# Block-diagonal v for the strided heads of an attention and expert kernel

## Chip, cores and metric

The kernel runs on one core of a Trainium2 chip. The time is device microseconds of one execution, and the median of several runs counts. Engines are called as in the profile: PE is TensorE (PEld its weight loads), DVE VectorE, ACT ScalarE, POOL GpSimd, SP SyncE, which here issues most DMAs.

## What is computed

Attention over 4 sequences of 576 positions with 8 heads of 64 (4 heads with a local mask of 32 positions, 4 with a strided mask), then a layer that sends each of the 2304 tokens to one of 8 experts, then a dense feed-forward layer:

```python
mask_local = (rel >= 0) & (rel < stride)
mask_strided = (rel >= 0) & (pos[None, :] % stride == pos[:, None] % stride)
masks = np.stack([mask_local if h < H // 2 else mask_strided for h in range(H)], axis=0)
scores = np.where(masks[None, :, :, :], scores, -1000000000.0)
...
x = np.ascontiguousarray(attn_out.transpose(0, 2, 1, 3)).reshape(B * S, H * D)
x = _moe_ref(x=x, **moe_kwargs)
return _moe2_ref(x=x, **moe2_kwargs)
```

All matmuls of the attention are in f32.

## The kernel before

The attention stage is one loop over 40 units, `for k in range(NU)` in `attention_and_routing`: 22 units of the strided heads, then 18 of the local ones. A pass k of the loop works on several units at once, as in a pipeline. It makes the scores of unit k (`stage_s`: mask matmuls, line 194, and score matmuls, line 207), the transposes of the probabilities of unit k-2 (`stage_t`, 236), the matmuls with v of unit k-3 (`stage_v`, 253 strided, 264 local), on DVE the division by the sums of unit k-4 (`v_norm1` to `v_norm3`) and the transposes of the result of unit k-5 (`stage_x`, 317). From pass 29 on the gate products of two tiles of tokens are added (`products`, 358). PE takes these in the order of the code.

A strided unit has 2 groups of 54 positions (`SR`; 3 columns of 18 positions that see each other) and 4 heads, which stand as two pairs `pr` with two heads `par` each. The transposed probabilities `pt` hold the keys of pair 0 in rows 0 to 63 and those of pair 1 in rows 64 to 127. `stage_v` runs one matmul for every `par`, `pr` and group: 54 rows, 64 columns of PE, 65 columns of v (64 and a column of ones that gives the sum).

Ahead of the scores of a unit stand matmuls on a tile `warm` whose result nobody reads (line 192): `KEEP0` gives their number for passes 0 to 10, `KEEP` that for later ones, 1 for a strided unit and 0 for a local one.

q with k, and v, come in by DMAs that SP issues in the order of the code, one of each for a group of one or two units (`load_qk`, `load_v`, called by `loads_to`, at every pass for `NLD - 1` groups ahead). A DMA waits until its buffer is free, and those behind it on SP wait too. POOL clears `x2t`, loads the constants of the routing (`load_consts`, called in pass 3) and then stores the strided results to DRAM (`store`, 310); the local results are stored by SP (302) once all loads are issued. Behind the loop come the routing, the experts and the feed-forward layer, which the change leaves alone.

Of the kernel before, what the change touches and what calls it, by code (L numbers as in the profile page):

```python
# [8 lines left out]
F32 = mybir.dt.float32  # L9
# [10 lines left out]
NE, FF, F2 = 8, 1024, 2048  # L20
# [20 lines left out]
NCV = 4  # L41
XR = 4
KEEP_R = (7, 9, 9)
NXN = 15
ST0 = 12
KEEP_D = 2
KEEP_X = 5
EARLY0 = (0, 0)
NOH = (3, 7)
QB = 32  # L50
QL = 2 * 256 + 2 * (256 + QB)
KEEP = {"s": 1, "l": 0}
KEEP0 = {0: 0, 1: 4, 2: 4, 3: 4, 4: 4, 5: 4, 6: 3, 7: 3, 8: 3, 9: 2, 10: 2}
NWM = 4
NLD = 9
NWS = 3
N_LOC = 8

# [27 lines left out]
def attention_and_routing(es, tc, a, x1, res):  # L86
    nc = tc.nc
    sy, ac, ve, gp, pe = nc.sync, nc.scalar, nc.vector, nc.gpsimd, nc.tensor
# [3 lines left out]
    cst = es.enter_context(tc.tile_pool(name="a_cst", bufs=1))  # L92
    ld = es.enter_context(tc.tile_pool(name="a_ld", bufs=NLD))
    wk = es.enter_context(tc.tile_pool(name="a_wk", bufs=3))
# [20 lines left out]
    mloc = cst.tile([128, 3, 64], BF16, name="mloc")  # L115
    mstr = cst.tile([128, 64], BF16, name="mstr")
    wg = cst.tile([128, 4, 32], F32, name="wg")
    fold = cst.tile([128, NE], F32, name="fold")
# [9 lines left out]
    groups, gof = [], {}  # L128
    for kind, sizes in (("s", (1, 1, 1, 1) + (2,) * 9), ("l", (2,) * 9)):
        t0 = 0  # L130
# [4 lines left out]
    for gi, (kind, t0, n) in enumerate(groups):  # L135
        for t in range(t0, t0 + n):
            gof[kind, t] = (gi, t - t0)
    qk_t, v_t = {}, {}

    def load_qk(gi):  # L140
        kind, t0, n = groups[gi]
        t = ld.tile([128, QL], F32, tag="qk", name="qk")
        if kind == "s":
            sy.dma_start(out=t[:, 0:n * 4 * SU], in_=a["qks"][:, t0:t0 + n, :].rearrange("p t c -> p (t c)"))
        else:
            sy.dma_start(out=t, in_=a["qkl"][:, t0 // 2, :])
        qk_t[gi] = t

    def load_v(gi):
        kind, t0, n = groups[gi]  # L150
        v = ld.tile([128, 4, 4, 66], F32, tag="v", name="v")
        vf = v.rearrange("p i h d -> p (i h d)")
        if kind == "s":
            sy.dma_start(out=vf[:, 0:264 * n], in_=a["vs"][:, t0:t0 + n, :].rearrange("p t c -> p (t c)"))
        else:
            sy.dma_start(out=vf[:, 0:528 * n], in_=a["vl"][:, 4 * t0:4 * t0 + 4 * n, :].rearrange("p i c -> p (i c)"))
        v_t[gi] = v

# [2 lines left out]
    def loads_to(k):  # L161
        while ngl[0] <= min(k, len(groups)):
            gi = ngl[0]
            if gi < len(groups):
                load_qk(gi)
            if gi > 0:
                load_v(gi - 1)
            ngl[0] += 1

    def geom(k):  # L170
        kind, t = units[k]
        gi, o = gof[kind, t]
        if kind == "s":
            return kind, t, 128 if t < NST - 1 else 64, 64, gi, o
        return kind, t, 128, 64, gi, o

    st = {}

    def sgroups(t):
        return [(g, min(SR, NT - t * SU - g * SR)) for g in range(2) if t * SU + g * SR < NT]  # L180

    def stage_s(k):
# [7 lines left out]
        mk = mk.unsqueeze(1).to_broadcast([128, 2, w])  # L190
        for i in range(KEEP0.get(k, KEEP[kind])):
            pe.matmul(sp[:, i % 2, 256:512], lhsT=warm[:, 0:128], rhs=warm[:, 0:256], start=True, stop=True)
# [23 lines left out]
    def v_max(k):  # L216
        kind, t, n, w, gi, o = geom(k)
        mx = wk.tile([128, 2, 2], F32, tag="mx", name="mx")
        ve.tensor_reduce(out=mx[0:n], in_=st[k, "s"], axis=AX.X, op=ALU.max)
        st[k, "m"] = mx  # L220
# [20 lines left out]
    def stage_v(k, xp=None):  # L241
        kind, t, n, w, gi, o = geom(k)
        pt = st.pop((k, "t"))
        v = v_t[gi]
        if xp is None:
            xp = ps.tile([128, 2, 512], F32, tag="xp", name="xp", bufs=1)
        st[k, "v"] = xp[0:n, :, 0:132].rearrange("p a (b c) -> p a b c", b=2)
        if kind == "s":
            for par in range(2):
                for pr in range(2):  # L250
                    for g, m in sgroups(t):
                        p0 = 64 * pr
                        pe.matmul(  # L253
                            xp[64 * g:64 * g + 64, pr, 66 * par:66 * par + 65],
                            lhsT=pt[p0:p0 + m, par, 64 * g:64 * g + 64], rhs=v[p0:p0 + m, o, 2 * g + par, 0:65],
                            start=True, stop=True,
                        )
            return
        v = v.rearrange("p i h d -> p (i h) d")
        for par in range(2):  # L260
            for pr in range(2):
                for j in range(4):
                    p0 = 64 * pr
                    pe.matmul(
                        xp[QB * j:QB * j + QB, pr, 66 * par:66 * par + 65],
                        lhsT=pt[p0:p0 + 64, par, QB * j:QB * j + QB], rhs=v[p0:p0 + 64, 8 * o + 2 * j + par, 0:65],
                        start=True, stop=True,
                    )
# [11 lines left out]
    def v_norm3(k):  # L280
        kind, t, n, w, gi, o = geom(k)
        xn = wk.tile([128, 256], F32, tag="xn", name="xn", bufs=NXN)
        ve.tensor_tensor(
# [14 lines left out]
    def store():  # L298
        k, xn = stores.pop(0)
        kind, t = geom(k)[0:2]  # L300
        if kind == "l":
            sy.dma_start(out=x1[t * 128:t * 128 + 128, 0:256], in_=xn)
        else:
            for g, rows in sgroups(t):
                c, p = 2 * t * CT + g * CT, 64 * g
                end = p + rows
                while p < end:
                    m = min((end - p) // NJ, STRIDE - c % STRIDE)
                    dst = x1.rearrange("(b j r) f -> b r j f", j=NJ, r=STRIDE)[c // STRIDE, c % STRIDE:c % STRIDE + m]
                    gp.dma_start(out=dst[:, :, 256:512], in_=xn[p:p + m * NJ])  # L310
                    c, p = c + m, p + m * NJ
# [54 lines left out]
    def folds(p, dst):  # L366
        t0, t1, lt = p
        for i in range(t1 - t0):
            pe.matmul(dst[:, NE * i:NE * i + NE], lhsT=lt[:, 128 * i:128 * i + 128], rhs=fold, start=True, stop=True)
        return t0, t1, dst[:, 0:NE * (t1 - t0)]  # L370
# [3 lines left out]
    def add(p):  # L374
        rt.add(*p)
        n_add[0] = p[1]

    def features(k):

        xq = bank("xq")  # L380
        t0 = lg_done[0]
        t1 = min(t0 + 2, lg_ready(max(0, k)))
        if t1 > t0 + 1:
            products(t0, t1, xq[:, 256:512])
        stage_x(k, xq)
        if t1 > t0 + 1:
            lt_p.append(fetch(t0, t1, xq[:, 256:512]))
            lg_done[0] = t1
# [2 lines left out]
    ve.memset(wg, 0.0)  # L391
    gp.memset(res["x2t"], 0.0)
    ve.memset(sc1, 0.0)
    loads_to(0)
    sy.dma_start(out=mstr, in_=a["mstr"])
    sy.dma_start(out=identb, in_=a["identb"])
    load_qk(1)
    sy.dma_start(out=ident, in_=a["ident"])
    load_v(0)
    ngl[0] = 2  # L400
    loads_to(3)
    sy.dma_start(out=mloc, in_=a["mloc"])
    sy.dma_start(out=wg[:, :, 0:NE], in_=a["w_gate"].rearrange("(c p) e -> p c e", p=128))
    sy.dma_start(out=fold, in_=a["fold"])
    ac.activation(out=sc1, in_=sc1, func=AF.Exp)
    wu = bank("xp")
    for i in range(9):
# [2 lines left out]
    LT, LV, LN, LX = 2, 3, 4, 5  # L410
    todo = []

    def side(n):
        while n and todo:
            if next(todo[0], todo) is todo:
                todo.pop(0)
            else:
                n -= 1

    def norm(u):  # L420
        v_norm1(u)
        v_norm2(u)
        v_norm3(u)

    loc = 0
    for k in range(NU):
        if k >= LN:
            norm(k - LN)
        side(1)
        loads_to(geom(k)[4] + NLD - 1)  # L430
        for _ in range(2):
            if k >= ST0 and len(stores) > 1 and (units[stores[0][0]][0] == "s" or ngl[0] > len(groups)):
                store()
        sp = stage_s(k)
        fd = folds(lt_p.pop(0), sp[:, 0, 192:256]) if lt_p else None
        v_max(k)
        if fd:
            add(fd)
        side(1)
        if k >= LX:  # L440
            features(k - LX)
        if k >= LT:
            stage_t(k - LT)
        side(1)
        v_sub(k)
        side(1)
        if k >= LV:
            stage_v(k - LV)
        if k == 3:
            rt.load_consts()  # L450
        if k == 8:
            rt.bias()
        if loc == 0 and n_add[0] >= N_LOC:
            todo += [rt.local(0, N_LOC), rt.gates(0, N_LOC)]
            loc = N_LOC
# [20 lines left out]
    stage_t(L - 1, bank("pp"))  # L476
    stage_x(L - 4, bank("xq"), True)
    stage_v(L - 2, pair("w1"))
    stage_t(L, bank("a0"))
    norm(L - 2)  # L480
# [9 lines left out]
    t0, t1 = lg_done[0], NTL - 4  # L490
# [1311 lines left out]
```

## Time and profile before

| | us |
|---|---|
| median of 3 runs (lowest, highest) | 727.0 (726.27, 728.14) |
| the profiled execution | 728.09 |
| its span, first to last instruction | 726.3 |
| PE busy in the span | 702.6 (97%) |
| DVE, ACT, POOL busy | 516.6, 407.0, 151.6 |
| mean granted clock of PE | 0.987 |

Times in the rows below are microseconds from the span's start. Busy times overlap, as the engines work side by side. A busy PE is not PE at its peak, since the ends of its matmuls are modelled. "Issue" in the chain of waits is time in which an engine waited for nothing that the profile shows. DMA share is the mean busy share of the 16 DMA engines; it can read a little over 1.

### The profile page before, as it was taken

To read this page: it belongs to the slowest core of one execution; us is meant where nothing else is said; L and a number is where in the kernel's file an instruction comes from. 1 tells how busy PE (TensorE), PEld (TensorE's weight loads), DVE (VectorE), ACT (ScalarE), POOL (GpSimd) and SP (SyncE) were. 2 spreads that over 40 slices of the span, in tenths; PEclk is the share of its full clock that TensorE was granted. 3 is DMA by queue.
4 is the path that set the end of the run, shared out by engine and by line. 5 is a ranking of instruction groups with operands and counts; after the bars stand their busy time and mean duration, and the time that the engine had idled before them with its cause. 6 is when DMAs were issued, how large, how long until landed. Compare 5 with 4: busy or idle time off the path is not lost.

```text
span 726.3 us, 15653 instructions
## 1 busy us (share of the span) xinstructions
PE 702.6 (97%) x6012; PEld 653.0 (90%) x6012; DVE 516.6 (71%) x1021; ACT 407.0 (56%) x791; POOL 151.6 (21%) x215
## 2 busy tenths in 40 slices
PE   8898997999999999999999999999999999999995
PEld 5665656999999989999999999999999999999995
DVE  5667776678868778775567899847747796773784
ACT  3455445545565466544566776657627746663761
POOL 7651013102320241021002444540000004000004
PEclk9879999999999999999999999999999999999998
DMA  8994118557686598455145799998887879878832
GB/s 257 390 382 156 59 39 264 202 191 230 232 288 196 175 312 304 159 176 216 38 163 166 272 333 357 366 323 256 250 247 247 256 234 328 254 247 245 258 90 88
DMA packets 69422, 167.90 MB, mean 231 GB/s; under 512 B 11064, under 2 KB 14552, under 8 KB 69344
## 3 DMA queue, kind: packets, MB, share of 16 engines
q1 hardware_dynamic: 53312, 125.14, 53.5%
q0 software_dynamic: 16032, 41.73, 16.0%
q8 instruction: 49, 0.80, 0.5%
q14 instruction: 29, 0.24, 0.1%
HBM read 128.00 MB, written 38.80 MB: 230 GB/s over the span
## 4 chain that ended last, share of the span: by engine, by line
PE 91%; DMA 2%; issue 2%; DVE 2%; POOL 1%; ACT 1%; SPq 0%; another core or an unknown queue 0%; POOLq 0%; ACTq 0%; DVEq 0%
PE hp L878 14%; PE yp L889 14%; PE fhp L1154 9%; PE op L1175 9%; PE lb L1472 7%; PE mb L1545 7%; PE md L1472 5%; PE la L1472 5%; PE md L1545 4%; PE ma L1545 4%; PE sp L207 2%; PE xq L317 2%; PE xp L253 1%; PE pp L236 1%; POOL out_dram L1182 1%
## 5 line engine op out<-in xcount | busy, mean ns | idle before, releaser
L848 DVE TENSOR_TENSOR w<-stg,w 128x1024 fp32r<-128x1024 f32 x56 | 68.4, 1223 | 43.1 <-ACT w L844 43.0
L844 ACT ACTIVATE w<-stg 128x1024 fp32r<-128x1024 f32 x56 | 59.2, 1059 | 70.3 <-PE yp L889 45.3
L878 PE MATMUL hp<-xh,w 128*128 128x384 f32 (+1 forms) x448 | 92.4, 328 | 1.9 <-ACT xh L870 0.7
L878 PEld LDWEIGHTS hp<-xh,w 128*128 128x128 f32 x448 | 76.7, 188 | 3.8 <-ACT w L844 1.3
L889 PE MATMUL yp<-hh,w 128*128 128x384 f32 x384 | 76.2, 340 | 0.0
L1154 PE MATMUL fhp<-xh,w 128*128 128x384 f32 x256 | 70.5, 336 | 0.0
L889 PEld LDWEIGHTS yp<-hh,w 128*128 128x128 f32 x384 | 66.9, 188 | 0.0
L1182 POOL DMA_INDIRECT out_dram<-x2t,idn x12 | 14.0, 1168 | 220.2 <-DVE x2t L1447 218.3
L1472 PE MATMUL lb<-xh,ws 128*128 128x384 f32 x192 | 55.0, 337 | 0.0
L1200 POOL DMA_DIRECT2D wd<-w x48 | 34.4, 897 | 88.5 <-DVE w L999 85.5
L1175 PE MATMUL op<-w,gh 128*128 128x512 f32 x192 | 49.1, 391 | 0.0
L1521 DVE TENSOR_TENSOR gl<-g,gh 128x384 fp32r<-128x384 f32 x64 | 33.5, 556 | 21.0 <-ACT gh L1520 21.0
L1154 PEld LDWEIGHTS fhp<-xh,w 128*128 128x128 f32 x256 | 46.7, 188 | 1.2
L878 PE MATMUL hp<-xl,w 128*128 128x384 f32 (+1 forms) x224 | 46.3, 328 | 0.0
L1154 PE MATMUL fhp<-xl,w 128*128 128x384 f32 x128 | 43.2, 338 | 0.0
L881 ACT ACTIVATE hh<-hp 128x384 fp32r<-128x384 f32 (+1 forms) x56 | 25.5, 456 | 31.1 <-PE hp L878 30.7
L1450 ACT ACTIVATE g<-g 128x384 f32<-128x384 f32 x48 | 25.1, 522 | 32.0 <-DVE g L1447 31.8
L1520 ACT ACTIVATE gh<-g 128x384 fp32r<-128x384 f32 x64 | 32.6, 523 | 16.4 <-PE mb L1545 8.2
L889 PE MATMUL yp<-hl,w 128*128 128x384 f32 x192 | 41.1, 336 | 0.0
L1175 PEld LDWEIGHTS op<-w,gh 128*128 128x128 f32 x192 | 35.6, 188 | 5.4
L878 PEld LDWEIGHTS hp<-xl,w 128*128 128x128 f32 x224 | 39.1, 188 | 0.0
L1545 PE MATMUL mb<-ws,gh 128*128 128x256 f32 x264 | 38.6, 282 | 0.5 <-ACT gh L1520 0.5
(299 smaller groups left out, 1723.1 us busy)
## 6 DMA issues: line engine op xcount, KB each, us to landing
ws<-wd SPq DMA_DIRECT2D x112, 512.0 KB, 4.5
stg<-in_wcat_dram SPq DMA_DIRECT2D x56, 512.0 KB, 4.0
stg<-in_w2cat_dram SPq DMA_DIRECT2D x32, 512.0 KB, 5.3
wd<-w POOLq DMA_DIRECT2D x48, 256.0 KB, 6.1
wd<-co POOLq DMA_DIRECT2D x16, 512.0 KB, 4.1
wd<-co POOLq DMA_DIRECT2D x32, 256.0 KB, 5.1
qk<-in_qkl_dram SPq DMA_DIRECT2D x9, 544.0 KB, 9.7
v<-in_vl_dram SPq DMA_DIRECT2D x9, 528.0 KB, 8.2
```

The costliest lines, as they stand in the source:

```text
L844: ac.activation(out=w[:, 0, :], in_=t, func=AF.Copy)
L848: ve.tensor_tensor(out=w[:, 1, :], in0=t, in1=w[:, 0, :].bitcast(F32), op=ALU.subtract)
L878: pe.matmul(hp, lhsT=w[:, wi, 128 * k:128 * k + 128], rhs=x[:, k, 0:n], start=(i == 0), stop=(i == 11))
L881: ac.activation(out=hh, in_=hp, func=AF.Relu)
L889: pe.matmul(yp[c][:, 0:SLOT], lhsT=w[:, wi, 512 + 128 * c:640 + 128 * c], rhs=x, start=(j == 0 and x is hh and wi == 0), stop=(j == NC1 - ...
L1154: pe.matmul(hp, lhsT=w[:, v, 128 * k:128 * k + 128], rhs=xs[ch, k // 2][xv][:, k % 2, :], start=(i == 0), stop=(i == 11))
L1175: pe.matmul(ops[ch][t], lhsT=x[:, 128 * t:128 * t + 128], rhs=w[:, v, :], start=(j == ORD[0] and first), stop=(j == ORD[-1] and last))
L1200: gp.dma_start(out=wd[lay, p // 4, 7 * (p % 4) + unit[lay][i]], in_=src)
L1472: pe.matmul(M[m], lhsT=w[:, v, k, :], rhs=xp_c[c][x][xv][:, k, :], start=(i < 3 and n == 0), stop=(n == 5), skip_group_check=True)
L1520: ac.activation(out=gh, in_=src, func=AF.Copy)
L1521: ve.tensor_tensor(out=gl, in0=src, in1=gh.bitcast(F32), op=ALU.subtract)
L1545: pe.matmul(at[t], lhsT=x[:, 128 * t:128 * t + 128], rhs=w[:, v], start=(new and e == 0 and x is gh and v == 0 and first), stop=(e == 3 an ...
```

## The change

The strided units get a v that is twice as wide: four tiles `vd` of 128 rows, each cleared once, in which the rows of pair 0 are loaded to the first half of the columns and those of pair 1 to the second half. One matmul then takes all 128 rows and gives both pairs, 2 x 65 columns. So `stage_v` has four matmuls for a strided unit instead of eight. Each strided v load becomes two DMAs of 64 rows.

Beside it: no warm matmul for strided units behind pass 10; strided v loads beyond the first four groups are issued by `loads_vs`, after the v matmuls of the group four before; qk and local v are loaded 3 to 7 groups ahead, more with the passes, instead of 8; the constants mloc, wg and fold are loaded by POOL in pass 3 instead of by SP at the start; 8 buffers for qk, 7 for local v (9 of each before), 13 for the result xn (15); stores from pass 8 on instead of 12.

```diff
-NXN = 15
-ST0 = 12
+NXN = 13
+ST0 = 8
...
-KEEP = {"s": 1, "l": 0}
+KEEP = {"s": 0, "l": 0}
...
-NLD = 9
+NLD = 8
+NLV = 7
+NVD = 4
...
+    vd = [cst.tile([128, 2, 2, 4, 66], F32, name=f"vd{i}") for i in range(NVD)]
...
         if kind == "s":
-            sy.dma_start(out=vf[:, 0:264 * n], in_=a["vs"][:, t0:t0 + n, :].rearrange("p t c -> p (t c)"))
+            v = vd[gi % NVD]
+            for pr in range(2):
+                r0 = 64 * pr
+                sy.dma_start(out=v[r0:r0 + 64, pr, 0:n].rearrange("p t h d -> p (t h d)"),
+                             in_=a["vs"][r0:r0 + 64, t0:t0 + n, :].rearrange("p t c -> p (t c)"))
...
-            if gi > 0:
+            if gi > 0 and (groups[gi - 1][0] == "l" or gi <= NVD):
                 load_v(gi - 1)
             ngl[0] += 1
+
+    nvs = [NVD]
+
+    def loads_vs(u):
+        while groups[nvs[0]][0] == "s" and sum(g[2] for g in groups[:nvs[0] - NVD + 1]) <= u + 1:
+            load_v(nvs[0])
+            nvs[0] += 1
...
+        if kind == "s":
+            x4 = xp[:, 0, 0:264].rearrange("p (a b c) -> p a b c", a=2, b=2)
+            for par in range(2):
+                for g, m in sgroups(t):
+                    p0 = 64 * g
+                    pe.matmul(x4[p0:p0 + 64, :, par, 0:65], lhsT=pt[:, par, p0:p0 + 64],
+                              rhs=v[:, :, o, 2 * g + par, 0:65], start=True, stop=True)
+            st[k, "v"] = x4[0:n]
+            return
         st[k, "v"] = xp[0:n, :, 0:132].rearrange("p a (b c) -> p a b c", b=2)
-        if kind == "s":
-            for par in range(2):
-                for pr in range(2):
-                    for g, m in sgroups(t):
-                        p0 = 64 * pr
-                        pe.matmul(
-                            xp[64 * g:64 * g + 64, pr, 66 * par:66 * par + 65],
-                            lhsT=pt[p0:p0 + m, par, 64 * g:64 * g + 64], rhs=v[p0:p0 + m, o, 2 * g + par, 0:65],
-                            start=True, stop=True,
-                        )
-            return
...
+    for v in vd:
+        ve.memset(v.rearrange("p a t h d -> p (a t h d)"), 0.0)
...
-    sy.dma_start(out=mloc, in_=a["mloc"])
-    sy.dma_start(out=wg[:, :, 0:NE], in_=a["w_gate"].rearrange("(c p) e -> p c e", p=128))
-    sy.dma_start(out=fold, in_=a["fold"])
...
-        loads_to(geom(k)[4] + NLD - 1)
+        loads_to(geom(k)[4] + min(NLD - 1, 3 + k // 2))
...
             stage_v(k - LV)
+            loads_vs(k - LV)
         if k == 3:
             rt.load_consts()
+            gp.dma_start(out=mloc, in_=a["mloc"])
+            gp.dma_start(out=wg[:, :, 0:NE], in_=a["w_gate"].rearrange("(c p) e -> p c e", p=128))
+            gp.dma_start(out=fold, in_=a["fold"])
```

The order of a strided pass on PE, behind pass 10. A row is a line, an operation, the tiles and the size; `xp` is the result of the v matmuls, `sp` the scores, `xq` and `pp` the transposes. Before:

```order
L192 LDWEIGHTS warm
L192 MATMUL sp<-warm 128x256
L194 LDWEIGHTS identb
L194 MATMUL sp<-mstr,identb 128x128
L194 LDWEIGHTS identb
L194 MATMUL sp<-mstr,identb 128x128
L207 MATMUL sp<-qk 54x54 x8
L317 MATMUL xq<-ident,xn 128x128 x2
L236 MATMUL pp<-ident,sm 128x128 x2
L253 MATMUL xp<-v,pt 64x65 x8
```

The same pass with the change:

```order
L208 LDWEIGHTS identb
L208 MATMUL sp<-mstr,identb 128x128
L208 LDWEIGHTS identb
L208 MATMUL sp<-mstr,identb 128x128
L221 MATMUL sp<-qk 54x54 x8
L329 MATMUL xq<-ident,xn 128x128 x2
L250 MATMUL pp<-ident,sm 128x128 x2
L266 MATMUL xp<-vd_96,pt 64x2x65 x4
```

The pair of the warm tile is gone, and eight matmuls with v became four of twice the columns.

The first DMAs on SP, up to the first load of two units (128x864). Before:

```order
L144 DMA qk<-in_qks_dram 128x432
L154 DMA v<-in_vs_dram 128x264
L402 DMA mloc<-in_mloc_dram 128x192
L403 DMA wg<-in_w_gate_dram 128x4x8
L404 DMA fold<-in_fold_dram 128x8
L144 DMA qk<-in_qks_dram 128x864
```

With the change:

```order
L147 DMA qk<-in_qks_dram 128x432
L158 DMA vd_96<-in_vs_dram 64x264 x2
L147 DMA qk<-in_qks_dram 128x864
L158 DMA vd_97<-in_vs_dram 64x264 x2
L147 DMA qk<-in_qks_dram 128x864 x3
L158 DMA vd_94<-in_vs_dram 64x528 x2
```

The three constants have left SP, the v loads stand there twice, and behind the fourth group v comes later than the qk loads of three groups.

## Rows read from the trace of the kernel before

**Rows 1.** Busy time by stretch: us, busy (instructions) by engine, granted PE clock, DMA share, GB/s

```profile
32.00:45.40 13.40, 13.40 (x195) 9.68 (x191) 8.04 (x26) 5.50 (x21) 8.03 (x14) 0.50 1.04 392
45.40:58.00 12.60, 11.12 (x293) 7.91 (x300) 9.51 (x33) 7.79 (x28) 7.77 (x14) 1.00 1.02 366
58.00:75.00 17.00, 15.29 (x573) 10.28 (x581) 11.84 (x41) 8.24 (x26) 0.72 (x2) 1.00 0.32 99
```

**Rows 2.** Chain that ended last, 0 to 70 us: start, us, what

```profile
6.96 5.09 DMA qk<-in_qks_dram
...
22.52 0.34 issue
...
28.37 1.90 issue
...
51.53 1.08 issue
...
57.04 0.39 issue
...
60.84 0.38 issue
```

**Rows 3.** Busy time by stretch, between waits; PE first, then PEld

```profile
22.86:28.25 5.39, 5.39 (x125) 4.12 (x125) 4.35 (x15) 2.93 (x13) 3.39 (x6) 1.00 1.08 386
46.43:51.40 4.97, 4.97 (x132) 3.73 (x133) 4.45 (x16) 3.30 (x13) 3.13 (x6) 1.00 1.06 382
57.43:60.70 3.27, 3.27 (x126) 2.29 (x126) 2.59 (x9) 1.79 (x7) 1.29 (x3) 1.00 0.79 221
```

**Rows 4.** DMA queues, 27.5 to 28.4 us: packets, MB, share of 16 engines

```profile
q8 instruction: 1, 0.02, 7.5%
```

**Rows 5.** Time line of PE around passes 10, 19, 20, 22, 25, 26

```profile
23.47 0.28 PE L194 MATMUL sp<-mstr,identb 128*128 128x128 bf16 x2
...
47.66 0.28 PE L192 MATMUL sp<-warm 128*128 128x256 bf16 x1
47.78 0.28 PE L194 MATMUL sp<-mstr,identb 128*128 128x128 bf16 x2
...
49.44 0.28 PE L194 MATMUL sp<-mstr,identb 128*128 128x128 bf16 x2
...
50.89 0.29 PE L194 MATMUL sp<-mloc,identb 128*128 128x128 bf16 x2
...
57.70 0.28 PE L194 MATMUL sp<-mloc,identb 128*128 128x128 bf16 x2
...
59.27 0.28 PE L194 MATMUL sp<-mloc,identb 128*128 128x128 bf16 x2
```

**Rows 6.** Chain that ended last, 0 to 70 us: v matmuls and gate products

```profile
34.66 0.64 PE xp L253 x16
...
37.45 0.64 PE xp L253 x16
...
48.99 0.39 PE xp L253 x16
...
62.76 0.39 PE xp L264 x32
...
66.19 0.57 PE xq L358 x8
```

**Rows 7.** Time line of SP at the start

```profile
6.42 0.50 SPq L404 DMA_DIRECT2D fold<-in_fold_dram  x1
```

**Rows 8.** Time line of DVE, 0 to 6 us; in brackets its idle time before

```profile
0.86 0.27 DVE L390 MEMSET warm<- 128x256 uint32 x1 [0.86 <-PEq L1790]
1.11 0.17 DVE L391 MEMSET wg<- 128x128 f32 x1
...
5.43 0.42 DVE L219 TENSOR_REDUCE mx<-sp 128x4 f32<-128x256 f32 x1 [4.15 <-PE sp L207]
```

**Rows 9.** DMA issues, 0 to 60 us: queue, count, KB, median us to landing

```profile
v<-in_vs_dram SPq DMA_DIRECT2D x9, 264.0 KB, 8.5
```

More of the change, by code (lines that the diff above doesn't have):

```diff
@@ L150, in load_v @@
         kind, t0, n = groups[gi]
-        v = ld.tile([128, 4, 4, 66], F32, tag="v", name="v")
-        vf = v.rearrange("p i h d -> p (i h d)")
         if kind == "s":
-            sy.dma_start(out=vf[:, 0:264 * n], in_=a["vs"][:, t0:t0 + n, :].rearrange("p t c -> p (t c)"))
-        else:
+            v = vd[gi % NVD]
[3 more added lines that the diff above has]
+                             in_=a["vs"][r0:r0 + 64, t0:t0 + n, :].rearrange("p t c -> p (t c)"))
+        else:
+            v = ld.tile([128, 4, 4, 66], F32, tag="v", name="v", bufs=NLV)
+            vf = v.rearrange("p i h d -> p (i h d)")
             sy.dma_start(out=vf[:, 0:528 * n], in_=a["vl"][:, 4 * t0:4 * t0 + 4 * n, :].rearrange("p i c -> p (i c)"))
```

## Prediction

> **What bounds the kernel now.** I read the stretches first, then the chain of waits, then the time line of TensorE (PE) inside the attention stage. The change touches nothing behind that stage, whose last pass ends near 92 us, and everything behind it (routing, the experts, the FFN) follows it in one chain. So the question is how much earlier the 40 passes end.
>
> [...] The chain of waits [rows 2] is PE throughout, with one DMA wait at the start (the fifth qk load, until 12.05) and then pieces called "issue", in which PE waits for nothing that the profile names: 0.34, 1.90, 1.08, 0.39, 0.38 us. Between such waits PE and its weight loads execute 125 + 125, 132 + 133 and 126 + 126 instructions [rows 3], always about 256. And the DMA table shows a queue "instruction" that moves one packet of 0.02 MB just ahead of the 1.90 us wait [rows 4]. I read this as PE running out of instructions at the end of each page of 256, until the next page has come. From one resumption to the next a page took 22.86 to 30.27 = 7.4 us and, from the page's first instruction at 46.43, 6.2 us to 52.61 with the DMA engines full, but 57.43 to 61.22 = 3.8 us with them nearly free [rows 2, 3]. Where DMA is full, then, PE can do 256 instructions in 6.2 to 7.4 us, 6.8 in the middle, whatever they are.
>
> **The change part by part.**
>
> Instructions of a strided pass. Before, a pass k of 11 to 21 issues 2 (warm) + 4 (masks) + 32 (scores) + 8 (transposes) + 32 (v) = 78 PE instructions, as an f32 matmul on a tile is two weight loads and two matmuls. With four v matmuls for eight and no warm one it is 60. A page then holds 4.27 passes for 3.28.
>
> PE's own time of a strided pass. It is 47.78 to 49.44 = 1.66 us now [rows 5]. The warm matmul takes 47.66 to 47.78 = 0.12 of it, 11 times. For the v matmuls, a pass takes 0.39 us now (16 passes over 65 columns on 64-column tiles, so 8 x 65 = 520 columns for each half of PE's columns) [rows 6]. After: 2 matmuls x 2 x 130 = 520 columns for each half, all 128 rows at once. If only the columns count, 0.39 again. The nearest row with 128 rows on narrow tiles is the gate product, 512 columns for each quarter in 0.57 us [rows 6]. I take 0.39, near the local units' v matmuls (32 instructions on 32-column tiles, also 520 columns each, also 0.39 [rows 6]), and keep 0.57 for the range. So a pass is 1.66 - 0.12 = 1.54; a local pass without warm matmuls took 57.70 to 59.27 = 1.57 [rows 5].
>
> [...]
>
> The strided passes. Pass 10 begins at 23.47 and pass 22 at 50.89 [rows 5]: 27.4 us for 12 passes, 2.28 each, of which 13.4 us lie in the half clock and 1.90 in one wait. After, 256 / 60 passes take max(4.27 x 1.54 = 6.6, 6.8), 1.60 a pass, 19.2 us (18.5 where PE alone counts, 20.9 at 7.4 us a page). The wait of 0.34 ahead of pass 10 goes, as the v steps of passes 3 to 9 are shorter by 112 instructions. Pass 22 begins at 23.1 + 19.2 = 42.3 (41.6 to 44.0).
>
> What is late next: DMA. The bytes are the same, and the engines were full until 58. So in the passes 22 and on, which issue 92 instructions (140 from pass 25 on, when v is local too), a page still costs 6.8 us until 58. 15.7 us make 2.31 pages = 591 instructions: three passes of 92, then 315 / 140 = 2.25. Pass 27.25 stands at 58.0. Before, pass 26 began at 59.27 and a pass took 3.8 x 140 / 256 = 2.07, so pass 27.25 stood at 61.9. **Gain 3.9 us** (5.1 at 6.2 us a page with pass 22 at 41.6; 2.3 at 7.4 us with 44.0). More than half of the 8.6 us gained by pass 22 is given back to the full DMA engines.
>
> The clock. The half clock set in within 2 us after the 1.90 us wait had ended at 30.27 [rows 1, 2]. In the pages between 42 and 58 PE needs 2.9 to 4.4 us for 256 instructions, so waits of 2.4 to 3.9 us stand there, and I expect one stretch of 13.4 us at half clock there too. A strided pass took 34.66 to 37.45 = 2.79 in it [rows 6], 1.68 times the full one; a local one would be 1.57 x 1.68 = 2.64, less than the 6.8 x 140 / 256 = 3.7 of the page. So only what lies behind 58 costs, 13.4 x (1 - 1 / 1.68) = 5.4 us if all of it, 0 if none. I take 1.0, about 2.5 us of it behind 58.
>
> The start. The fifth qk load is the 14th issue on SP before and after: mloc, wg and fold leave (0.50 for the last [rows 7]) and three second halves of v come. The third and fourth qk loads are later by one and two issues, which the wait until 12.05 [rows 2] covers. Its data have three small loads less ahead of them. I take 0; +0.5 to -1.0.
>
> The memsets of vd on DVE: (0.27 - 0.17) / 128 = 0.78 ns an element, so 4 x 0.9 = 3.6 us from 1.28, until 4.9; DVE idles until 5.43 [rows 8]. Cost 0; if it were slower, DVE's first maximum would move by the excess.
>
> The v loads, four groups ahead, now wait for the v step four groups before. Seven passes of 1.6 us are 11.2 us against 8.5 us to landing with DMA full [rows 9]. Cost 0, to 0.5 where a landing is some us over that median. Behind a waiting v load on SP stand the qk loads of passes 14 and more ahead, so that costs nothing. The three constants on GpSimd stand ahead of its x1 stores and are first read in pass 22. The smaller pools (8 qk, 7 v, 13 xn buffers) and stores from pass 8 on leave all of this in order: cost 0.
>
> Sum: -3.9 (pages, warm matmuls, strided clock) + 1.0 (clock later) = -2.9. The profiled execution took 728.09 us and its span was 726.3; the median of the runs is 727.0. The sum is a difference within the span, so it comes off the median: **724.1 us**. What measurement can tell from no change is 0.3%, or 2.2 us: faster is below 724.8, slower above 729.2.
>
> **The rivals.**
>
> A. No half clock at all, and pages of 6.2 us. For it: with 60 instructions a pass, PE (6.6) is hardly faster than a page, so the first long wait may not come. Against: the local passes. 727.0 - 5.1 = 721.9.
>
> [...]
>
> C. **Slower**: a second stretch of half clock, behind 58, where no page hides it. The pass without its warm matmul leaves PE with fewer matmuls, and waits of over 2 us come in rows. Price: 5.4 us beside the 1.0 of the first: -3.9 + 1.0 + 5.4 = +2.5, 729.5. It decides once more than 3.9 / 0.40 = 10 us of half clock lie behind 58. Against it: from 58 to 75 the waits are 0.4 us and the clock stayed at 1.00 without a warm matmul [rows 1, 2].
>
> D. The pages don't bound: the waits have another cause, and fewer instructions change nothing in them. The change then gives only 11 x 0.12 = 1.3 us, 725.7. [...]
>
> **How the numbers follow.** Forecast 0.38, with its own range of 722.5 to 725.6 from the bounds of gain and clock; A 0.22, D 0.13, B 0.10, C 0.17. Faster: 0.29 of the forecast, all of A, 0.01 of D, 0.52. Slower: 0.12 of C and 0.03 of B (0.57 or more, and a stretch of clock), 0.15. Same: the rest, 0.33. The range of 8 in 10 reaches from 720.8, a little under A, to 729.5, C.
>
> **What would show it.** Right: waits called "issue" of well under 1.9 us in the strided passes, every 4.3 passes; the local passes beginning near 42 us with DMA still full, then waits of 2 us and more at every page until 58; the attention stage 3 us shorter. Wrong: a v step well over 0.39; PE waiting for vd; waits that don't come every 256 instructions; or a granted clock of 0.50 behind 58.

## The result, and the profile after

| | before | after |
|---|---|---|
| median of 4 runs (lowest, highest), us | 727.57 (726.27, 728.15) | 737.38 (734.43, 738.88) |
| the profiled execution, its span, us | 728.09, 726.3 | 738.88, 737.1 |
| mean granted clock of PE | 0.987 | 0.980 |

The change is slower: ratio 1.0132, 95% interval 1.0095 to 1.0169. The prediction was 724.1 us, and its range ended at 729.5. The profiled execution after is the slowest of its four, so its trace shows a little more than the median's loss.

First the stretches after, as [rows 1] gave them before, with one ahead of them and one behind (us, busy time and instructions by engine from PE to POOL, granted PE clock, DMA share, GB/s):

```profile
15.00:30.00 15.00, 13.20 (x195) 9.40 (x192) 9.24 (x30) 6.28 (x26) 9.55 (x18) 0.89 1.07 302
32.00:45.40 13.40, 12.09 (x210) 8.43 (x204) 10.76 (x36) 8.34 (x31) 6.39 (x11) 1.00 1.07 299
45.40:58.00 12.60, 9.05 (x148) 6.08 (x150) 6.36 (x21) 5.21 (x18) 6.72 (x12) 0.86 1.07 314
58.00:75.00 17.00, 13.68 (x368) 8.94 (x368) 8.88 (x29) 5.53 (x17) 3.54 (x6) 0.72 0.68 239
...
116.70:123.50 6.80, 6.47 (x20) 3.61 (x21) 4.50 (x17) 1.77 (x2) 3.72 (x3) 0.50 0.70 231
```

From 32 to 45.4 the DMA engines are as full as before, a share of 1.07 for 1.04 [rows 1]. But they move 299 GB/s there where they moved 392, and 314 up to 58 for 366. Behind 58, where they had been nearly idle (0.32), they still work at 0.68. The long half clock of 32 to 45.4 (0.50 in [rows 1]) is gone, as foreseen; shorter pieces stand elsewhere: ahead of 30 (0.89 in the mean), behind 45.4 (0.86), from 58 to 75 for more than half of the time (0.72), and once at 116.7.

What the DMA engines moved from 15 to 45 us, in the DMA view; before:

```profile
DMA packets 5846, 11.77 MB, mean 392 GB/s; under 512 B 2418, under 2 KB 2418, under 8 KB 5840
```

After:

```profile
GB/s 399 381 263 231 287 273 330 391 324 268 245 263 249 273 337 384 278 293 274 296 350 394 345 269 247 333 347 393 344 259 238 243 279 294 382 382 288 256 234 264
DMA packets 5076, 9.14 MB, mean 305 GB/s; under 512 B 2292, under 2 KB 2308, under 8 KB 5071
```

By 45 us the engines have moved 2.63 MB less since 15; at 392 GB/s that is 6.7 us of work for full engines. The first line gives the rate in 40 equal slices: it is not lower all along, but swings between 231 and 399 GB/s, as it would if the loads on half of the rows were slow and those between them were not. No row says which load was moving in a slice.

Who waited after, 0 to 110 us (engine, line, for what: us in total, times, longest):

```profile
PE xp L266 <- DMA vd<-in_vs_dram: 6.6, 5, 1.9
...
PE sp L221 <- issue: 3.8, 3, 2.7
```

PE now waits for v itself, which it did not before. The time line of PE shows where, with the passes that answer to [rows 5] (start, us, what; in brackets the idle time before):

```profile
27.05 0.28 PE L208 MATMUL sp<-mstr,identb 128*128 128x128 bf16 x2
...
28.19 0.66 PE L266 MATMUL xp<-vd,pt 128*64 128x130 f32 x8
28.79 0.29 PE L208 MATMUL sp<-mstr,identb 128*128 128x128 bf16 x2
...
52.94 0.28 PE L208 MATMUL sp<-mloc,identb 128*128 128x128 bf16 x2
...
57.80 0.67 PE L266 MATMUL xp<-vd,pt 128*64 128x130 f32 x8 [1.44 <-DMA vd<-in_vs_dram]
...
69.08 0.42 PE L221 MATMUL sp<-qk 64*32 64x64 f32 x2 [2.69 <-issue]
...
96.35 0.28 PE L208 MATMUL sp<-mloc,identb 128*128 128x128 bf16 x2
```

Pass 10 begins at 27.05 (before 23.47 [rows 5]), pass 22 at 52.94 (50.89; forecast 42.3), pass 39, the last, at 96.35 (89.09 before). One strided pass takes 28.79 - 27.05 = 1.74, and its v step 28.19 to 28.79 = 0.60, where before it was 0.39 [rows 6]. So 7.3 us are lost when the loop ends. The first matmul of the experts stands at 128.56 against 119.86, 8.7 later, with the piece of half clock at 116.7 between; what makes 8.7 into the 10.8 us of the spans lies behind it and was not followed.

The tile vd (duration min/median/max in ns; first and last start):

```profile
L266 PE MATMUL xp<-vd,pt x172: 272/273/481, 10.0 to 61.0; 128*64 128x130 f32 x172
...
L407 DVE MEMSET vd<- x4: 938/938/938, 1.4 to 4.8; 128x1056 f32 x4
```

The memsets take 0.94 each, near the estimate. With 0.17 idle ahead of each the last one starts at 4.77, and DVE's first maximum starts at 5.63 instead of 5.43 [rows 8].

### The profile page after: what moved, and what is told of

It is laid out like the page before. It is cut to its first block, busy times and chain, and to the rows that moved or that the text cites. A ratio compares the mean times of both kernels' runs of the same rounds, so it can differ in the third digit from the quotient of the medians.

```text
span 737.1 us, 15320 instructions
## 1 busy us (share of the span) xinstructions
PE 709.0 (96%) x5827; PEld 655.4 (89%) x5829; DVE 520.6 (71%) x1025; ACT 407.7 (55%) x791; POOL 154.3 (21%) x218
## 4 chain that ended last, share of the span: by engine, by line
PE 78%; ACT 1%; POOL 1%; DMA 1%; issue 1%; DVE 1%; POOLq 0%; ACTq 0%; DVEq 0%
PE hp L893 14%; PE yp L904 14%; PE fhp L1169 9%; PE op L1190 9%; PE lb L1487 7%; PE mb L1560 6%; PE md L1487 5%; PE la L1487 5%; PE md L1560 4%; PE ma L1560 4%; PE tp L882 1%; DMA stg<-in_wcat_dram 1%; POOL out_dram L1197 1%; ACT xg L877 0%; ACT w L859 0%
```

## The experiments

The main theory (H below): v in two DMAs of 64 neighbouring rows lowers the rate of the full DMA engines, and all else (v and qk late, waits, half clock) follows. Its rivals: the dearer v step, 0.60 for 0.39, is the loss (M); the missing warm matmul brings the half clock; the loads are issued at the wrong time (O). A ratio is to the kernel before, run beside it. There is one trace of each kernel; its times in the attention stage are those of one execution.

**The DMA alone, in the kernel before.** Three kernels split each strided v load in two: by neighbouring rows (e1, the diff), by columns `c0:c0 + 132 * n` of all rows (e2), and by even and odd rows `r0:128:2` (e5).

```diff
-            sy.dma_start(out=vf[:, 0:264 * n], in_=a["vs"][:, t0:t0 + n, :].rearrange("p t c -> p (t c)"))
+            for r0 in (0, 64):
+                sy.dma_start(out=vf[r0:r0 + 64, 0:264 * n],
+                             in_=a["vs"][r0:r0 + 64, t0:t0 + n, :].rearrange("p t c -> p (t c)"))
```

> The kernel before, with each strided v load issued as two DMAs of 64 neighbouring rows, as in the changed kernel, and nothing else of the change. Theory H (half rows): in the changed kernel the DMA engines, just as full as before (share 1.07), moved only about 300 GB/s where they moved 390, since the DMAs of 64 rows slow each other and everything beside them. H expects about 310 GB/s between 15 and 45 us here too, the loads done some 5 us later than at 58, and 731 to 735 us. Theory M (the v matmuls on 128 rows take 0.60 us for 0.39) and theory O (v is loaded too late, four groups ahead and behind the local loads) expect no change here, 727 to 728 us and 390 GB/s.

> The kernel before, with each strided v load issued as two DMAs of all 128 rows and half the columns: as many DMAs as in the run on half rows, as many bytes, but shorter pieces of each row. H, if it is the 64 rows: 380 to 390 GB/s, 727 to 729 us. H, if it is the number of DMAs or of issues on SP: as slow as the half rows. M and O: 727 to 728 us.

> The kernel before, with each strided v load as two DMAs of 64 rows again, but of every other row (the even ones, then the odd ones) instead of the lower and the upper half. If it is that neighbouring rows of one half of the memory are written alone (H, adjacency), the rate stays near 385 GB/s and the time at 727 to 730 us. If any DMA of 64 rows slows the transfers, 270 to 310 GB/s and 735 to 740 us, as with the half rows (739.06 us).

Half rows: 739.06 us (734.71 to 740.48), ratio 1.0152 (1.0106 to 1.0199). Half columns: 730.13, 1.0028 (1.0004 to 1.0052). Even and odd rows: 733.63, 1.0071 (1.0037 to 1.0105). The DMA view, 15 to 45 us, of the half rows:

```profile
DMA packets 4769, 8.06 MB, mean 269 GB/s; under 512 B 2088, under 2 KB 2088, under 8 KB 4765
```

of the half columns:

```profile
DMA packets 7322, 11.42 MB, mean 381 GB/s; under 512 B 2739, under 2 KB 4992, under 8 KB 7316
```

and of the even and odd rows:

```profile
DMA packets 5826, 10.88 MB, mean 363 GB/s; under 512 B 2479, under 2 KB 2479, under 8 KB 5820
```

Twice the DMAs and smaller packets cost little (0.3%); two loads of 64 neighbouring rows alone lose as much as the whole change. The size is near one simple estimate from the 392 GB/s: if a half-row load is taken to run at half of that, a strided group of 432 KB of qk and 264 KB of v takes 1.10 + 1.35 us, or 284 GB/s in the mean; 269 were moved. The half is an assumption; no row shows the rate of one load. The chain of waits of the half-row kernel then shows the rest (start, us, what):

```profile
9.55 4.25 DMA qk<-in_qks_dram
...
25.70 1.04 issue
...
32.25 3.27 issue
...
56.72 1.63 issue
```

A wait for issue of 3.27 stands where before the longest was 1.90 [rows 2]. Instruction packets take time of the same 16 DMA engines, 7.5% of it from 27.5 to 28.4, just ahead of that 1.90 [rows 4]; that behind the 3.27 a packet came late is a reading. Even and odd rows missed the 727 to 730 us expected of them. By 45 us they are 0.89 MB behind, 2.3 us at 392 GB/s, for a loss of 5.2 us, so the rate alone does not explain it. The wait for the fifth qk load lasts until 13.8 (12.05 before [rows 2]), and a half clock (0.50) fell on 45.4 to 58. So in the kernel before, about half of the 1.5% of the half rows stays when the rows are spread, and why is open.

**The same repair in the changed kernel (e6).** The two heads of a pair stand on even and odd rows, so each DMA writes 64 rows spread over all 128. The DMAs read the same DRAM rows as in the change; only the rows of SBUF differ, and DVE writes the probabilities interleaved to match. All other parts of the change stay in.

```diff
-                sy.dma_start(out=v[r0:r0 + 64, pr, 0:n].rearrange("p t h d -> p (t h d)"),
+                sy.dma_start(out=v[pr:128:2, pr, 0:n].rearrange("p t h d -> p (t h d)"),
...
-        sm4 = sm.rearrange("p (a b w) -> p a b w", a=2, b=2)[0:n]
+        lay = "p (a w b) -> p a b w" if kind == "s" else "p (a b w) -> p a b w"
+        sm4 = sm.rearrange(lay, a=2, b=2)[0:n]
```

> The changed kernel with the two pairs of heads on even and odd rows instead of the lower and upper half: DVE writes the probabilities with the pairs interleaved, and the v loads go to every other row. Bytes, number of DMAs, order of the loads and the PE instructions are those of the changed kernel. H, adjacency: 380 GB/s again and most of the loss gone, 727 to 732 us; what then stays above 727.4 belongs to the v step of 0.60 us and to the loads' order. O (v is loaded too late): the waits for v stay, 734 us and more. If any DMA of 64 rows is slow: no change, 737 us.

728.61 us (727.18 to 731.39), ratio 1.0006 (0.9982 to 1.0031): the whole loss of the change is gone, with the v step at 0.60, no warm matmul and the same order of the loads. Its DMA view, 15 to 45 us:

```profile
DMA packets 6208, 11.39 MB, mean 380 GB/s; under 512 B 2815, under 2 KB 2831, under 8 KB 6202
```

Its waits for v, of 6.6 us after:

```profile
PE xp L267 <- DMA vd<-in_vs_dram: 1.0, 2, 0.7
```

Its stretches, and the 3.6 us between its two long waits:

```profile
15.00:30.00 15.00, 13.86 (x229) 10.05 (x225) 10.96 (x36) 7.66 (x31) 10.87 (x21) 1.00 1.05 372
32.00:45.40 13.40, 13.40 (x228) 9.54 (x228) 11.66 (x40) 8.90 (x33) 9.40 (x17) 1.00 1.06 388
45.40:58.00 12.60, 10.28 (x283) 6.86 (x284) 8.16 (x27) 6.26 (x23) 5.72 (x10) 0.93 1.04 388
58.00:75.00 17.00, 15.56 (x494) 10.06 (x486) 10.56 (x36) 6.99 (x21) 0.00 (x0) 0.75 0.46 138
...
55.36:58.98 3.62, 3.62 (x127) 2.26 (x127) 2.27 (x8) 0.98 (x3) 0.33 (x1) 0.62 0.91 331
```

Its chain of waits:

```profile
53.42 1.94 issue
...
58.98 1.44 issue
```

Here the strided passes run without page waits, as the prediction had them: PE never waits from 32 to 45.4, clock 1.00. Part of that is luck: with the dearer v step a page, taken as 256 instructions, lasts 4.27 x 1.74 = 7.4 us on PE, not 6.6, which is as long as the slowest page of [rows 2, 3]. Pass 22 begins at 45.88, 5.0 us earlier than before. One trace of each makes that gain uncertain: with look-ahead alone changed (e9, below), which left the rate at 392 GB/s, pass 22 begins at 48.5. Then the local passes meet DMA engines that are still full: waits of 1.94 and 1.44 us, 254 instructions apart, and the half clock behind them. Pass 39 begins at 87.36, 1.7 us earlier than before (89.06 with the order of the v matmuls alone changed, e8 below, and 87.80 in e9). Even that does not arrive. The chain of waits before, at the routing and at the first matmul of the experts:

```profile
107.51 2.87 issue
...
119.86 5.15 PE hp L878 x28
```

and with even and odd rows:

```profile
106.51 2.87 issue
...
119.76 5.30 PE hp L894 x29
```

1.0 us earlier at the first and 0.1 at the second. Between them, from 114 to 118, PE had a granted clock of 0.57 on even and odd rows and 1.00 before; whether that is the 0.9 us was not followed.

**One DMA of 128 rows, with the zeros in DRAM.** Twice the bytes of v, no memsets; the layout of the input has the zero blocks, and no arithmetic is left out.

```diff
-            for pr in range(2):
-                r0 = 64 * pr
-                sy.dma_start(out=v[r0:r0 + 64, pr, 0:n].rearrange("p t h d -> p (t h d)"),
-                             in_=a["vs"][r0:r0 + 64, t0:t0 + n, :].rearrange("p t c -> p (t c)"))
+            sy.dma_start(out=v[:, :, 0:n].rearrange("p a t h d -> p a (t h d)"),
+                         in_=a["vs"][:, :, t0:t0 + n, :].rearrange("p a t c -> p a (t c)"))
...
```

> The changed kernel with v laid out block-diagonally in DRAM, zeros included, and loaded by one DMA of 128 rows: twice the bytes for v (some 3 MB more, 7 us of full DMA), no clearing of the tiles. H: 380 to 390 GB/s again, waits for v mostly gone, 729 to 734 us. M and O: at least 737 us, as v comes no sooner and more is to be moved.

738.44 us, ratio 1.0138 (1.0084 to 1.0192). Its DMA view, 15 to 45 us:

```profile
DMA packets 6324, 11.51 MB, mean 384 GB/s; under 512 B 2526, under 2 KB 2542, under 8 KB 6319
```

One DMA of 128 rows gives the rate back, 384 GB/s, as H has it. But the time missed H's 729 to 734 us and is the one that M and O had (at least 737): the 3 MB of zeros are some 7.7 us of full engines at this rate, and PE waits 6.0 us for vd. That more bytes at the full rate lose like the same bytes at a lower one is argued from that sum; no run shows it alone.

**The v step.** The changed kernel with eight matmuls of 64-row tiles again, on the new vd; and the kernel before with its eight matmuls in another order, row half first, so that neighbours in the order no longer lie in different row halves.

```diff
...
-                for g, m in sgroups(t):
-                    p0 = 64 * g
-                    pe.matmul(x4[p0:p0 + 64, :, par, 0:65], lhsT=pt[:, par, p0:p0 + 64],
-                              rhs=v[:, :, o, 2 * g + par, 0:65], start=True, stop=True)
+                for pr in range(2):
+                    for g, m in sgroups(t):
+                        p0 = 64 * pr
+                        pe.matmul(xp[64 * g:64 * g + 64, pr, 66 * par:66 * par + 65],
+                                  lhsT=pt[p0:p0 + m, par, 64 * g:64 * g + 64],
+                                  rhs=v[p0:p0 + m, pr, o, 2 * g + par, 0:65], start=True, stop=True)
...
```

> The changed kernel with its loads as they are, but the v step again as eight matmuls of 64-row tiles (0.39 us for 0.60, and 32 PE instructions for 16). M: 22 steps by 0.21 us, 4.6 us less, near 733 us. H and O: PE only comes sooner to loads and instruction pages that are late anyway; less than 2 us gained, 735.5 to 739 us.

> The kernel before, with the eight v matmuls of a strided unit in another order: all four on the rows of pair 0, then all four on those of pair 1, where before the row half changed after every second one. It asks why the v step on 128 rows took 0.60 us and not 0.39. If weights can be loaded beside a running matmul only in rows that it does not use, the step becomes longer here, 0.45 to 0.60 us, as the row half changes once instead of three times. If only the columns count, 0.39. Time within 2 us of before in both cases.

The first: 737.34 us, ratio 1.0139 (1.0102 to 1.0175), as slow as the change, though its v step is back at 0.39. Its stretches:

```profile
32.00:45.40 13.40, 10.08 (x222) 7.43 (x210) 8.41 (x29) 6.80 (x25) 7.22 (x12) 0.86 1.07 300
45.40:58.00 12.60, 12.60 (x186) 8.99 (x182) 7.96 (x25) 5.77 (x21) 6.43 (x11) 0.50 1.06 305
58.00:75.00 17.00, 17.00 (x408) 11.23 (x403) 10.58 (x34) 6.96 (x24) 4.42 (x8) 0.50 0.75 266
```

300 GB/s as after, and a half clock from 45.4 to 75. This is no clean price of the step: eight matmuls also put 16 PE instructions a pass back, and a wait for issue of 3.32 us stands at 39.88, ahead of that half clock. The cleaner case against M is the version on even and odd rows, which keeps the step of 0.60 and loses nothing against the kernel before. So the 0.21 us a pass are real, but they are not the loss. The second, in a single run of 726.8 us: the v step at full clock stands between these two rows of PE's time line, 0.41 (0.40 in the kernel before, read the same way):

```profile
23.31 0.48 PE L253 MATMUL xp<-v,pt 54*64 54x65 f32 x16
23.72 0.28 PE L192 MATMUL sp<-warm 128*128 128x256 bf16 x1
```

The order of the row halves made no difference here. Why four matmuls on 128 rows take 0.60 stays open.

**The warm matmul.** Taken out of passes 11 to 21 in the kernel before (`KEEP` 0), and put back in the changed kernel on even and odd rows (`KEEP` 1), the last twice.

> The kernel before without the warm matmul in the strided passes 11 to 21, and nothing else of the change. By the sum of the prediction 11 x 0.12 us and 22 PE instructions less: 0.5 to 2 us faster, 725.5 to 727. Theory C (the clock falls for want of matmuls): more or longer stretches at a granted clock of 0.50, 729 to 735 us.

> The changed kernel on even and odd rows with the warm matmul of passes 11 to 21 back. If PE time counts: 11 x 0.12 = 1.3 us slower than 728.6, 729 to 731 us. If the clock is what the warm matmul holds up, as in the kernel before without it (a stretch of 41 us at 0.50), it is 1 to 4 us faster, 724.5 to 727.5 us; but with the wider v step the clock stayed at 1.00 until 56 us without it, so the first is likelier.

> The changed kernel with pairs on even and odd rows and the warm matmul kept in passes 11 to 21, once more, beside the kernel before, to tell whether it is faster than the kernel before by what it was in the first comparison (0.26%). Buffers are left at 8 for qk and 7 for v. If it is a gain: ratio 0.995 to 0.999 again; if it was chance: 0.999 to 1.003.

Without it before: 730.74 us, ratio 1.0029 (0.9990 to 1.0069). The page wait and the stretches behind it; the chain of waits first:

```profile
26.65 1.93 issue
```

```profile
28.60:45.40 16.80, 16.80 (x251) 11.92 (x251) 10.43 (x33) 7.04 (x25) 10.26 (x18) 0.50 1.04 393
45.40:69.00 23.60, 23.60 (x489) 16.04 (x490) 14.69 (x47) 10.13 (x34) 8.59 (x15) 0.50 0.71 237
```

In this execution the half clock lasts from 28 to 69 instead of 32 to 45.4. Over all executions the mean granted clock was 0.974 without the warm matmul (ten) and 0.982 in the kernel before (21), so the half clock is longer without it. The 725.5 to 727 us expected of its absence did not come, but the time is not clearly longer either, and not by 10 us. On even and odd rows the clock stays at 1.00 until 56 without the warm matmul; the mean over the executions was 0.988 without it and 0.992 and 0.991 with it. With it: 727.98, ratio 0.9974 (0.9948 to 0.9999), and in the second comparison 728.22, ratio 1.0000 (0.9974 to 1.0026). The first gain was not confirmed: no version here is shown to beat the kernel before.

**Fewer loads ahead.** Four groups of look-ahead instead of 8 in the kernel before, of 3 to 7 on even and odd rows and in the change (`loads_to(geom(k)[4] + 4)`, or `min(4, 3 + k // 2)`).

> The kernel before with one number changed: loads 4 groups ahead instead of 8, so that the same bytes are spread over the whole attention stage and the DMA engines are not full until 58 us. It tests the step of the prediction on which the rest stands, that PE waits for instruction pages because the DMA engines are full. If so, the waits called issue fall to about 0.4 us in the strided passes as well, the clock keeps 1.00, and the stage ends 3 to 9 us earlier: 718 to 724 us. If the waits have another cause (rival D of the prediction), they stay, and the time is 726 to 729 us; if loads come late instead, 730 us and more.

> The changed kernel on even and odd rows (728.6 us) with loads at most 4 groups ahead instead of 7. If full DMA engines are what holds PE, 719 to 725 us. The v step of 0.60 us and the missing warm matmul set what it gains or loses against the kernel before with the same look-ahead: by PE time 22 x (0.20 - 0.06) = 3 us slower than that.

> The changed kernel itself (half rows) with loads at most 4 groups ahead instead of 7. If the loss of 64 neighbouring rows is one of transfer rate alone, it costs little once the engines are not full: 722 to 730 us, and fewer waits for v. If the half rows cost as much as before at the start, where everything is late, 732 us and more.

Before: 728.31, ratio 0.9977 (0.9949 to 1.0004), with the same 392 GB/s from 15 to 45: the edit missed its aim. SP issued the first load of local qk at 23.01 us, near pass 10 on PE, though it stands in pass 14 of the program; in the kernel before it was at 22.94. So the place in the program held nothing back; the 9 buffers were the same. On even and odd rows: 733.61, 1.0055 (1.0025 to 1.0084); with 308 GB/s pass 22 began at 45.79, as with 7 groups (45.88), but the loads came later, with engines full up to 68 us (share 0.69 from 58 to 75, for 0.46), and a wait for issue of 3.51 stood at 55.9. The change: 736.14, 1.0084 (1.0056 to 1.0112), still slower. The gain expected of the first two, to 718 to 725 us, did not come.

So buffers were taken away instead (`NLD` sets their number and the look-ahead): `NLD` 5 and 6 for 9 before, and 6 for qk and 5 for local v in the version with even and odd rows and the warm matmul.

> The kernel before with 5 buffers for each of qk and v instead of 9, so that a load really waits for the group five before it; nothing else is changed. Theory (full DMA engines hold PE at the end of a page of 256 instructions, with v loads of 128 rows as well): the engines move fewer GB/s up to pass 22, the waits called issue in the strided passes fall from 1.90 us to 0.4 to 0.6, no stretch at the half clock lies ahead of 45 us, pass 22 begins 3 us or more earlier; the load work that is put off comes back in the local passes, so 724 to 730 us. Rival (those waits are not due to the full DMA engines): the waits of 1.1 to 1.9 us stay where they were, every 256 instructions, and pass 22 stays near 50.9. If five buffers are too few, PE waits for qk or v: 731 us or more.

> The same with 6 buffers of each. Theory: between the kernel before and the one with 5 buffers in the rate of the DMA engines and in the waits called issue; 724 to 729 us. Rival: as before, 727 to 728, with the same waits.

> The same with 6 buffers for qk and 5 for local v. Theory (full DMA engines hold PE at pages): fewer and shorter issue waits in the strided passes, the load work later; 725 to 729 us. Rival (buffers are no lever, or too few of them make PE wait for loads): within 0.2% of the one with 8 and 7 buffers, or 730 us and more.

732.25, ratio 1.0053 (1.0022 to 1.0084); 729.25, 0.9989 (0.9949 to 1.0030); 729.45, 1.0015 (0.9982 to 1.0048). Only the first moved clearly, and it lost. Its pass 22 begins at 45.83, earlier than in the kernel before, as the theory had it; but the waits did not fall to 0.4 to 0.6 us, and a half clock still lies ahead of 45 us, both against it. It shows more of the pages. Its chain of waits:

```profile
26.29 1.63 issue
...
46.47 1.63 issue
...
67.34 0.55 issue
...
79.06 2.25 issue
```

the last 2 us ahead of each of the three long ones, for the DMA share, and the stretches between the waits:

```profile
24.29:26.29 2.00, 2.00 (x49) 1.45 (x50) 1.78 (x6) 1.47 (x7) 1.78 (x4) 1.00 1.06 365
44.50:46.47 1.97, 1.97 (x57) 1.34 (x55) 1.73 (x8) 1.50 (x6) 0.89 (x2) 1.00 1.01 361
77.06:79.06 2.00, 2.00 (x66) 1.48 (x64) 1.67 (x7) 1.16 (x4) 0.00 (x0) 1.00 1.07 385
...
27.92:46.47 18.55, 18.55 (x375) 13.59 (x375) 14.10 (x48) 10.22 (x37) 13.75 (x24) 0.82 0.87 259
48.10:67.34 19.24, 19.09 (x506) 12.38 (x505) 12.30 (x40) 8.71 (x29) 3.72 (x7) 0.65 0.83 274
67.89:79.06 11.17, 10.95 (x381) 7.52 (x382) 7.74 (x28) 5.71 (x17) 0.00 (x0) 1.00 0.61 187
```

The stretches hold 750, 1011 and 763 instructions, three, four and three pages if a page is the 250 to 265 of [rows 3]. Read so, the long waits still stand at ends of pages, and seven ends between them cost next to nothing (PE idle for 0, 0.15 and 0.22 us in the three stretches), in stretches whose DMA share is 0.61 to 0.87 in the mean. Each of the three long waits came behind 2 us of full engines, shares of 1.06, 1.01 and 1.07. This supports that full DMA engines make a page late; it does not say how full they must be, since on even and odd rows the wait of 1.44 at 58.98 ended a page with 0.91 in the mean and 0.79 in its last 2 us. And it gives no time: what is not loaded early is loaded later, in front of the local passes (a share of 0.83 from 48.1 to 67.34).

## Why the prediction was wrong

**What is late next: DMA.** Here it failed. The step reads "The bytes are the same, and the engines were full until 58", and goes on with 6.8 us a page until 58. The bytes were the same; the rate was not. 305 GB/s for 392 put the engines 6.7 us behind by 45 us, full engines lasted past 58, PE waited 6.6 us for v and 3.8 for issue, read as late pages, and the clock fell behind the waits. e1 (half rows in the kernel before) makes the loss with the DMAs alone, e6 (the change on even and odd rows) takes it away by the rows of SBUF.

**The v loads, cost 0, to 0.5.** The same error at its source. The step weighed when a load is issued and its landing time of 8.5 us [rows 9], which comes from loads of 128 rows. No row of before shows a load of 64 rows, so it had to be bounded from both sides; with half the rate, an assumption, as the lower bound the estimate above gives 284 GB/s. No rival held it either; C had the right sign but another cause. The runs gave 269 (e1) and 305 GB/s (after) with 64 neighbouring rows and 380 with every second row (e6), for 392 before; what makes the difference is not shown.

**PE's own time of a strided pass.** A term that was mis-sized: 0.39 was taken and 0.60 measured, just over the 0.57 kept for the range; a pass takes 1.74, not 1.54. Rival B, the v step at twice 0.39 or 0.78, had the sign: eight matmuls of 64 rows do gain on four of 128, by a factor of 1.5 and not of two. No run shows the doubling on which its chance of 0.10 rested, and why the factor is 1.5 is not shown either. In the change the step cannot be read apart from the loads (e3, the change with eight matmuls). In e6 it shows: the 19 v steps up to pass 21, 0.21 each, are 4.0 us, and its pass 22 (45.88) misses the forecast of 42.3 by 3.6.

**The strided passes and the pages.** Right where the loads come in time, with the luck named above: in e6 no wait for issue above 0.14 us and no half clock from 17 to 53 us. Rival D, that the pages don't bound, has against it that long waits stand 254 instructions apart in e6 and that in e13 (5 buffers) 750, 1011 and 763 stand between the three long ones and one of 0.55. The page itself is a reading of such counts, and so is its price of 6.2 to 7.4 us where DMA is full: the page of 3.8 us that the prediction has nearly free of DMA had a share of 0.79 [rows 3]. But the sum of that step was not reached by any version, since pass 22 came 8.6 us early in the forecast, 5.0 in e6, and 2.1 late after.

**Given back to DMA.** Right in kind, with the rate repaired: 5.0 us at pass 22 are 1.7 at pass 39 (forecast 8.6 and 3.9), in one trace of each. That the rest follows the last pass in one chain was not quite so: of 1.7 us 0.1 was left at the experts' first matmul.

**The clock.** The long stretch went, as forecast, and shorter ones came, the first ahead of 30 us behind a wait for v, the others behind 45.4. The 1.0 us named for it cannot be read apart from the late loads.

**The start, the memsets, the constants.** The memsets were sized right (0.94 each, forecast 0.9) and move DVE's first maximum by 0.2 us, not by nothing. The start does not hold: pass 10 begins 3.6 us later. Seven v steps ahead of it, 0.21 dearer each, are 1.5 of that, and e6, which has them too, begins pass 10 at 25.0, 1.5 later than before. The rest in the change goes with a wait for v and a half clock behind it, which is the low rate again.

## What to carry to other kernels

Splitting a transfer was not free here, where the DMA engines were full (shares of 1.02 and 1.04 [rows 1]): 64 neighbouring rows cost the kernel before 1.5%, every second row 0.7%, half the columns 0.3%. So look at which rows of SBUF each piece writes, and try a half load spread over all 128 rows; in the changed kernel that cost nothing (ratio 1.0006). Read the GB/s beside the DMA share: from 32 to 45.4 a share of 1.04 was 392 GB/s before, and one of 1.07 was 299 after. And in e6, with the DMA engines full to 58 (1.04), the 5.0 us gained at pass 22 were 1.7 at pass 39, with waits of 1.94 and 1.44 us between; so bound the new form of a load before counting instructions.

## What the runs showed of the hardware

- The rows that the v loads write change what the full DMA engines move in all, from 15 to 45 us: 392 GB/s with loads of 128 rows, 269 when the v loads became 64 neighbouring rows, 363 to 380 with every second row, 381 with two loads of 128 rows and half the columns.
- Four f32 matmuls of 128 rows, 64 columns of PE and 130 columns of v take 0.60 us; eight of 64 rows and 65 columns take 0.39, or 0.41 in the other order of the row halves. Filling the rows with zeros saved instructions and cost 0.21 us of PE.
- In one execution each, a wait of 1.93 us was followed by 40.4 us at a granted clock of 0.50 (28.6 to 69) without warm matmuls in passes 11 to 21 (e7), and one of 1.90 us by 13.4 us at 0.50 (32 to 45.4) with one a pass.
- With 5 buffers the three long waits for issue, 1.63, 1.63 and 2.25 us, came behind 2 us of full DMA engines (1.06, 1.01 and 1.07). Between them and one of 0.55 stood 750, 1011 and 763 PE instructions, three, four and three times about 252, in which PE was idle for 0, 0.15 and 0.22 us.
